# Key weights' low halves behind VectorE's low halves of x, a later table load, and z from two summed tiles

## The chip, the cores and the metric

The kernel runs on one core of a Trainium2 chip. The metric is the time of one execution on the device in microseconds (us), median of a few runs. TensorE multiplies matrices; VectorE, ScalarE and GpSimd work elementwise; SyncE (SP) issues most DMAs, GpSimd some. In the profile they are called PE (PEld: its weight loads), DVE, ACT, POOL and SP. Each engine runs its instructions in order.

## The reference

One transformer block with adaptive layer norm, 2048 rows of 512 numbers in 32 bits. What matters here is the first half:

```python
mod = (_silu(c) @ w_mod).reshape(c.shape[0], 6, 1, -1)
sa, ca, ga, sb, cb, gb = (mod[:, 0], mod[:, 1], mod[:, 2], mod[:, 3], mod[:, 4], mod[:, 5])
h = _layernorm(x, axis=-1) * (1 + ca) + sa
...
phi = lambda t: jnp.where(t > 0, t + 1, jnp.exp(t)) + 1e-6
pq, pk = phi(q), phi(k)
kv = jnp.einsum("bhsd,bhse->bhde", pk, v)
z = jnp.einsum("bhsd->bhd", pk)
num = jnp.einsum("bhqd,bhde->bhqe", pq, kv)
den = jnp.einsum("bhqd,bhd->bhq", pq, z)[..., None] + 1e-6
o = num / den
```

z is the sum of phi(k) over all 2048 rows. Behind this come the projection with wo, the residual, and a second layer norm with two dense layers and Mish, which the change doesn't touch.

## The kernel before

The 2048 rows are four blocks b of four tiles t of 128 rows; the 512 columns are four chunks k of 128. Every matmul operand is split into a high half (h) rounded to TensorE's fast 32-bit type and a low half (l), the remainder; a product takes three matmuls: high by high, high by low, low by high (mm3, L74 to L76). The order of instructions on each engine is the order in which the Python code writes them; waits between engines are put in from the data.

Block 0 is written out by hand (loop at L558 to L610). For each chunk k, ScalarE reads the transposed x from PSUM twice and writes hT_x_0_kh and hf_x_0_k, scaled and shifted by columns k and 4+k of `mc`. VectorE makes those columns with mod_col (L175) and plus_one (L179), and then the low half hT_x_0_kl (L590). GpSimd makes the key weights' halves wk_(k+1)h (a cast, L84) and wk_(k+1)l (a subtraction, L88) one behind the other. ScalarE loads the table that the exponential needs behind the first chunk (L582). TensorE takes hT and wk as they come and sums k = x wk into four PSUM tiles pk_0 to pk_3 (kp in the code).

From pk_t, k_post (L306) lets ScalarE make e_k and relu_k, VectorE ku = min(e_k, 1) + relu_k, and both the halves of ku as pk. g_unit (L327) multiplies normalized x by pk into four PSUM tiles gacc.

The tiles ku are also summed over the blocks for z. Before, four sums ku_0 to ku_3 grow: block 0's tiles are where they begin, blocks 1 and 2 add theirs by a DMA that accumulates in its target, issued by GpSimd (L313), and VectorE adds block 3's (L311). z_unit (L336) then multiplies the four sums by a tile of ones, 32 columns each, into four groups of 32 partitions of one PSUM tile; the two halves of that tile are multiplied by a constant 1/32 later (L683), which adds the partitions up.

Blocks 2 and 3 get x transposed another way: VectorE normalizes (L210) and turns 32 by 32 squares (wide_x, L239), four DMAs write them to DRAM (sq_x<-wide_x) and four read them back (sq_x<-sq_x), and ScalarE scales what comes (hf_x, L270). The layer norm's root is a power on GpSimd (rs_x, L199), between two VectorE steps (L194, and nb_x, L203). For block 3 this is written while block 1 is at work, and its rs_x stands on GpSimd behind the accumulating DMAs of block 1.

Of the kernel before, what the change touches and what calls it, by code (L numbers as in the profile page):

```python
# [13 lines left out]
P = 128  # L14
# [11 lines left out]
def block_kernel(ctx: ExitStack, tc: tile.TileContext, x, wqkv, wo, w1, b1t, w2, c, wmodt, out):  # L26
# [18 lines left out]
    def f32(t):  # L45
        return t.bitcast(F32)
# [21 lines left out]
    def run(gen):  # L68
        for _ in gen:
            pass  # L70

    def mm3(o, st, mv, start, stop):

        pe.matmul(o, st[0], mv[0], start=start, stop=False)  # L74
        pe.matmul(o, st[0], mv[1], start=False, stop=False)  # L75
        pe.matmul(o, st[1], mv[0], start=False, stop=stop)  # L76

    def split(name, t, keep, key, lo_engine=dve, hi_engine=act, plus=None):

# [63 lines left out]
    warm_up(3)  # L143
    ident = cst.tile([P, P], F32, name="ident")
    make_identity(nc, ident)
    w32 = cst.tile([P, P], F32R, name="w32")
    bmask = cst.tile([P, P], F32, name="bmask")
    hmask = cst.tile([P, 4, 32], F32, name="hmask")

    kv = sb("kv")  # L150

    def make_constants():
        pool.memset(f32(w32), 1.0 / 32)
        pool.memset(kv, 0.0)

        pool.memset(bmask, 1.0)
        bm3 = bmask.rearrange("p (a r) -> p a r", r=16)
        pool.affine_select(bm3, bm3, pattern=[[-16, 8], [0, 16]], compare_op=ALU.is_ge,
                           fill=0.0, base=0, channel_multiplier=1)
        pool.affine_select(bm3, bm3, pattern=[[16, 8], [0, 16]], compare_op=ALU.is_ge,  # L160
                           fill=0.0, base=15, channel_multiplier=-1)

        pool.memset(hmask, 1.0)
        pool.affine_select(hmask, hmask, pattern=[[128, 4], [-16, 32]], compare_op=ALU.is_ge,
                           fill=0.0, base=0, channel_multiplier=1)
        pool.affine_select(hmask, hmask, pattern=[[-128, 4], [16, 32]], compare_op=ALU.is_ge,
                           fill=0.0, base=15, channel_multiplier=-1)
# [138 lines left out]
    def k_post(p, b, t, hi_engine=act):  # L306
        u = ku[b, t] = sb(f"ku_{b}_{t}")
        yield from phi(p, f"k_{b}_{t}", u)
        yield from split(f"pk_{b}_{t}", u, pk, (b, t), hi_engine=hi_engine, plus=TINY)
        if b == NB - 1:  # L310
            dve.tensor_tensor(ku[0, t], ku[0, t], ku.pop((b, t)), op=ALU.add)  # L311
        elif b:
            pool.dma_start(ku[0, t], ku.pop((b, t)), accum_op=ALU.add)  # L313

    def k_unit(b, *tiles):
        p = {t: ps("h", f"pk_{b}_{t}") for t in tiles}
# [10 lines left out]
    def g_unit(b, t):  # L327
        if not gacc:
            gacc.extend(ps("acc", f"gacc_{k}") for k in range(4))
        for k in range(4):  # L330
            cs = slice(P * k, P * (k + 1))
            mm3(gacc[k], [h[:, cs] for h in xn[b, t]], pk[b, t], b == 0 and t == 0, b == NB - 1 and t == 3)

    zsum = [sb(f"zsum_{i}", F32R) for i in range(2)]

    def z_unit():  # L336

        p = ps("h", "z")
        for t in range(4):
            pe.matmul(p[32 * t:32 * (t + 1), :], ones[:, 0:32], ku.pop((0, t)), start=True, stop=True)  # L340
        act.activation(zsum[0], p, AF.Copy)
        dve.scalar_tensor_tensor(zsum[1], p, S * TINY / 4, f32(zsum[0]), op0=ALU.add, op1=ALU.subtract)

    def q_unit(b, g):
        p = ps("h", f"pq_{b}_{g}")
# [207 lines left out]
    def step(*gens):  # L553
        for g in gens:
            next(g, None)

    tss = [slice(P * t, P * (t + 1)) for t in range(4)]
    for k in range(4):  # L558
        hi, lo = sb(f"hT_x_0_{k}h", F32R), sb(f"hT_x_0_{k}l", F32R)
# [16 lines left out]
        else:  # L576
            upper(hi, 0, 512)
            upper(hf_k, 0, 512)
        if k < 3:
            run(split(f"wk_{k + 1}", wraw[1, k + 1], wk, k + 1, pool, pool))  # L580
        if k == 0:
            act.preload_act_table_set("exp_and_others")  # L582
            mod_pair(1)
        if k == 1:
            step(xsplit[0])
            mod_col(7, sc_bc)
            plus_one(7, 8)
        if k == 3:
            step(xsplit[0])
        dve.tensor_tensor(lo, hf_k, f32(hi), op=ALU.subtract)  # L590
        if k == 0:
            mod_pair(2)
        if k == 1:
            mod_col(3, sc_bc)
        if k == 0:

            for ts_ in (0, 1), (2, 3):
# [1039 lines left out]
```

## Time and profile before

| | |
|---|---|
| median of 3 runs | 483.81 us (483.48 to 484.19) |
| the profiled execution, whole | 483.39 us |
| its span, first to last instruction | 481.6 us |
| TensorE busy | 474.2 us, 98% of the span |
| VectorE, ScalarE, GpSimd busy | 393.5, 309.3, 128.9 us |
| chain that ended last, by engine | TensorE 85%, VectorE 7%, DMA 3%, ScalarE 2% |

A busy TensorE isn't a TensorE at its peak, since matmuls overlap and their ends are modelled: read the waits. The chain that ended last leads from engine to engine through what released each step. A landing time is that of a DMA from its issue to its last byte's signal.

### The profile page before, as it was taken

The numbers are of one execution on the slowest core, as the hardware profiler recorded it, in microseconds if no ns is written. First come the engines' busy times: TensorE is split into PE (matmuls) and PEld (weight loads), VectorE is DVE, ScalarE is ACT, GpSimd is POOL, SyncE is SP. The second block draws the span as 40 slices with busy tenths as digits, with TensorE's granted clock in tenths as the row PEclk, the third lists the DMA queues.
The fourth block names the chain that finished last, engine by engine and source line by source line (L and its number), as shares of the span: only waits on it lengthen the run. The fifth ranks groups of instructions, "written<-read, shape, count | busy, mean of one in ns | idle before, by whom it ended". The sixth has DMA issues, their size and how long they took to land.

```text
span 481.6 us, 7044 instructions
## 1 busy us (share of the span) xinstructions
PE 474.2 (98%) x2290; PEld 387.6 (80%) x2290; DVE 393.5 (82%) x785; ACT 309.3 (64%) x555; POOL 128.9 (27%) x216
## 2 busy tenths in 40 slices
PE   7999999999999999999999999999999999999997
PEld 6688877768887888788888888888888888888887
DVE  6899898999899889699779873799444787779992
ACT  6786468756667977587787756694166677537700
POOL 3673121000022254112223424343011101354400
PEclk9999999999999999999999999999999999999999
DMA  8904849543766246927538759999543503487964
GB/s 282 389 30 86 198 103 286 180 139 102 242 177 186 94 115 175 323 93 242 174 110 236 246 157 293 376 309 285 182 124 88 112 21 87 110 218 162 240 155 101
DMA packets 83839, 87.00 MB, mean 181 GB/s; under 512 B 23217, under 2 KB 57529, under 8 KB 83802
## 3 DMA queue, kind: packets, MB, share of 16 engines
q1 hardware_dynamic: 58248, 50.22, 34.9%
q0 software_dynamic: 23296, 35.54, 27.0%
q10 hardware_dynamic: 2258, 0.79, 0.7%
q8 instruction: 18, 0.29, 0.2%
q14 instruction: 19, 0.16, 0.1%
HBM read 57.42 MB, written 24.91 MB: 171 GB/s over the span
## 4 chain that ended last, share of the span: by engine, by line
PE 85%; DVE 7%; DMA 3%; ACT 2%; issue 1%; POOL 1%; SPq 0%; DVEq 0%; ACTq 0%
PE p_a L1205 15%; PE o L952 9%; PE p_s L1205 8%; PE oacc L75 5%; PE oacc L76 5%; PE oacc L74 5%; PE m L75 5%; PE m L74 5%; PE m L76 5%; PE p L1205 4%; PE pq_a L390 2%; PE pq L74 2%; DMA sq_x<-wide_x 2%; PE pq L75 2%; PE pq L76 2%; PE pk L76 1%
## 5 line engine op out<-in xcount | busy, mean ns | idle before, releaser
L1210 DVE TENSOR_TENSOR cb<-p_s,u 128x512 f32<-128x512 f32 x28 | 19.2, 687 | 12.2 <-ACT u L1258 10.7
L791 POOL DMA_DIRECT2D wb<-w2d x14 | 9.8, 705 | 65.1 <-PE m L76 28.3
L1197 ACT ACTIVATE ub<-cb,b1c 128x512 f32<-128x512 f32 x28 | 20.0, 719 | 9.0 <-DVE cb L1210 8.7
L1533 POOL DMA_DIRECT2D wt_m<-w2t x20 | 14.0, 702 | 25.2 <-PE m L76 16.9
L1215 ACT ACTIVATE p<-p_a 128x512 f32<-128x512 f32 x12 | 7.0, 582 | 20.9 <-PE p_a L1205 11.7
L199 POOL TENSOR_TENSOR rs_n<-rs_n,half 128x1 f32<-128x1 f32 x16 | 10.2, 636 | 36.9 <-DVE rs_n L225 19.1
L904 POOL DMA_DIRECT2D rden_d<-rden x2 | 1.5, 734 | 61.0 <-DVE rden L902 61.0
L1258 ACT ACTIVATE u<-p_a 128x512 f32<-128x512 f32 x14 | 8.4, 597 | 13.8 <-PE p_a L1205 13.6
L1172 ACT ACTIVATE u<-p,b1c 128x512 f32<-128x512 f32 x14 | 9.6, 685 | 11.7 <-PE p L1205 11.7
L1172 ACT ACTIVATE u<-p_a,b1c 128x512 f32<-128x512 f32 x14 | 9.6, 688 | 8.5 <-PE p_a L1205 8.3
L797 POOL DMA_DIRECT2D w2b<-w2d x20 | 10.6, 544 | 12.8 <-PE oacc L76 4.6
L304 DVE SCALAR_TENSOR_TENSOR ku<-e_k,relu_k 128x512 f32<-128x512 f32 x16 | 10.9, 684 | 1.9 <-ACT relu_k L302 1.9
L199 POOL TENSOR_TENSOR rs_x<-rs_x,half 128x1 f32<-128x1 f32 (+1 forms) x10 | 7.8, 785 | 15.8 <-DVE rs_x L194 14.9
L270 ACT ACTIVATE hf_n<-sq_n,mc 128x512 f32<-128x512 f32 x16 | 12.0, 802 | 0.0
L304 DVE SCALAR_TENSOR_TENSOR q<-e_q,relu_q 128x512 f32<-128x512 f32 x16 | 10.7, 688 | 1.4 <-ACT relu_q L302 1.4
L190 DVE BATCH_NORM_STATS2 st_x<-x 128x6 f32<-128x512 f32 x13 | 8.8, 676 | 3.0 <-DMA x<-in_x_dram 3.0
L301 ACT ACTIVATE e_k<-pk 128x512 f32<-128x512 f32 x16 | 9.4, 590 | 2.5 <-PE pk L76 2.5
L313 POOL DMA_DIRECT2D ku<-ku x8 | 7.2, 938 | 13.8 <-DVE ku L304 13.8
L256 POOL DMA_DIRECT2D sq_n<-wide_n x16 | 8.7, 554 | 7.2 <-DVE wide_n L239 4.7
L916 DVE SCALAR_TENSOR_TENSOR q<-q,rd 128x512 f32<-128x512 f32 x16 | 10.4, 684 | 0.3 <-DMA rd<-rden_d 0.3
L175 DVE SCALAR_TENSOR_TENSOR wm<-wm,sc_row 128x512 f32<-128x512 f32 x16 | 10.5, 685 | 0.0
L730 DVE TENSOR_TENSOR w2g<-w2r,gb_bc 128x256 f32<-128x256 f32 x28 | 10.0, 419 | 0.0
(1612 smaller groups left out, 1880.4 us busy)
## 6 DMA issues: line engine op xcount, KB each, us to landing
wm<-in_wmodt_dram SPq DMA_DIRECT2D x24, 256.0 KB
w1p<-in_w_dram SPq DMA_DIRECT2D x24, 256.0 KB
w2b<-w2d POOLq DMA_DIRECT2D x20, 256.0 KB, 7.3
wt_m<-w2t POOLq DMA_DIRECT2D x20, 256.0 KB, 3.6
r<-in_x_dram SPq DMA_DIRECT2D x16, 256.0 KB
x<-in_x_dram SPq DMA_DIRECT2D x15, 256.0 KB
w2r<-in_w_dram SPq DMA_DIRECT2D x14, 256.0 KB
wb<-w2d POOLq DMA_DIRECT2D x14, 256.0 KB, 3.4
```

Of the source, the lines that this page charges most:

```text
L74: pe.matmul(o, st[0], mv[0], start=start, stop=False)
L75: pe.matmul(o, st[0], mv[1], start=False, stop=False)
L76: pe.matmul(o, st[1], mv[0], start=False, stop=stop)
L199: pool.tensor_tensor(y, y, half[:, lo:hi], op=ALU.pow)
L270: act.activation(dst.rearrange("p (t a i) -> p t a i", t=4, a=4), turned.pop((key, b, j)).rearrange("p (a t i) -> p t a i", a=4, t=4), AF. ...
L304: dve.scalar_tensor_tensor(dst, e, 1.0, r, op0=ALU.min, op1=ALU.add)
L952: pe.matmul(p, l, r, start=not seeded and g == 0 and i == 0, stop=g == 3 and i == 2, skip_group_check=seeded)
L1172: act.activation(u, p, AF.Mish, bias=b1c[:, f:f + 1])
L1197: act.activation(u, p, AF.Mish, bias=b1c[:, f:f + 1])
L1205: pe.matmul(p, st, mv, start=onto is None and c == 0 and i == 0, stop=c == 1 and i == 2, skip_group_check=onto is not None)
L1210: dve.tensor_tensor(out, p, u, op=ALU.add)
L1533: pool.dma_start(v, w2t[g][:, :, SUM[name], :])
```

## The change

Five things. **Gates:** GpSimd's order in block 0 gets three copies of one element, `behind(lo)`, each reading a low half hT_x_0_kl that VectorE writes, so that what stands behind on GpSimd can't begin before that half is done. **Shares:** wk_2h goes from GpSimd to ScalarE, wk_3l from GpSimd to VectorE; xn_0h and xn_0l (halves of normalized x) and the scalings by `mc` move within their engines. **Table:** the load for the exponential moves behind ScalarE's reads of the last chunk. **First g_unit:** its twelve matmuls go over the four gacc tiles with one kind of half after the other, and those with pk_0l last. **z:** two sums grow instead of four. Block 0's tiles 2 and 3 are added by DMA too, tiles t and t + 2 of each block go to the same sum, z_unit has two matmuls of 64 columns, and the constant is 1/64.

```diff
@@ -308,9 +308,11 @@
         if b == NB - 1:
-            dve.tensor_tensor(ku[0, t], ku[0, t], ku.pop((b, t)), op=ALU.add)
+            dve.tensor_tensor(ku[0, t % 2], ku[0, t % 2], ku.pop((b, t)), op=ALU.add)
         elif b:
-            pool.dma_start(ku[0, t], ku.pop((b, t)), accum_op=ALU.add)
+            if b == 1 and t < 2:
+                pool.dma_start(ku[0, t], ku.pop((0, t + 2)), accum_op=ALU.add)
+            pool.dma_start(ku[0, t % 2], ku.pop((b, t)), accum_op=ALU.add)
...
+        if first:
+            (xh, xl), (ph, pl) = xn[b, t], pk[b, t]
+            for n, (l, r) in enumerate(((xh, ph), (xl, ph), (xh, pl))):
+                for k, cs in enumerate(css):
+                    pe.matmul(gacc[k], l[:, cs], r, start=n == 0, stop=False)
+            return
...
-        for t in range(4):
-            pe.matmul(p[32 * t:32 * (t + 1), :], ones[:, 0:32], ku.pop((0, t)), start=True, stop=True)
+        for t in range(2):
+            pe.matmul(p[64 * t:64 * (t + 1), :], ones[:, 0:64], ku.pop((0, t)), start=True, stop=True)
...
+    def behind(t):
+
+        pool.tensor_copy(gate, f32(t)[0:1, 0:1])
...
@@ -576,22 +601,30 @@
-        if k < 3:
-            run(split(f"wk_{k + 1}", wraw[1, k + 1], wk, k + 1, pool, pool))
         if k == 0:
-            act.preload_act_table_set("exp_and_others")
+            wk_upper(1, pool)
             mod_pair(1)
         if k == 1:
+            wk_upper(2, act)
+        if k == 2:
             step(xsplit[0])
-            mod_col(7, sc_bc)
-            plus_one(7, 8)
+        if k == 3:
+            act.preload_act_table_set("exp_and_others")
+        dve.tensor_tensor(lo, hf_k, f32(hi), op=ALU.subtract)
+        if k == 0:
+            behind(lo)
+            wk_lower(1, pool)
+            mod_pair(2)
+        if k == 1:
+            behind(lo)
+            wk_lower(2, pool)
+            wk_upper(3, pool)
+            mod_pair(3)
+        if k == 2:
+            wk_lower(3, dve)
         if k == 3:
             step(xsplit[0])
-        dve.tensor_tensor(lo, hf_k, f32(hi), op=ALU.subtract)
-        if k == 0:
-            mod_pair(2)
-        if k == 1:
-            mod_col(3, sc_bc)
+            behind(lo)
```

wk_upper and wk_lower write a chunk's high and low half of the key weights on the engine that they are given.

How the instructions stand, in three places. First GpSimd in block 0, before; a name in brackets is an engine or a DMA whose signal the instruction waits for:

```order
L84 CAST wk_1h<-wr_1_89 128x512 [waits DMAHW2_49]
L88 TENSOR_TENSOR wk_1l<-wr_1_89,wk_1h 128x512 [waits Pool_49]
L84 CAST wk_2h<-wr_2_95 128x512 [waits DMAHW5_49]
L88 TENSOR_TENSOR wk_2l<-wr_2_95,wk_2h 128x512 [waits Pool_49]
L84 CAST wk_3h<-wr_3_101 128x512 [waits DMAHW0_49]
L88 TENSOR_TENSOR wk_3l<-wr_3_101,wk_3h 128x512 [waits Pool_49]
L84 CAST xn_1h<-x_1_75 128x512 [waits Activation_49]
```

and GpSimd at the same place now:

```order
L577 CAST wk_1h<-wr_1_89 128x512 [waits DMAHW2_49]
L570 COPY gate<-hT_x_0l 1x1 [waits DVE_49]
L580 TENSOR_TENSOR wk_1l<-wr_1_89,wk_1h 128x512 [waits Pool_49]
L570 COPY gate<-hT_x_1l 1x1 [waits DVE_49,Pool_49]
L580 TENSOR_TENSOR wk_2l<-wr_2_95,wk_2h 128x512 [waits DMAHW5_49,Activation_49]
L577 CAST wk_3h<-wr_3_101 128x512 [waits DMAHW0_49]
L570 COPY gate<-hT_x_3l 1x1 [waits DVE_49,Pool_49]
L84 CAST xn_1h<-x_1_75 128x512
```

Each gate reads one of VectorE's low halves; wk_2h and wk_3l have left this engine.

Second, VectorE at the same place, from the low half of chunk 0 to that of chunk 3, before:

```order
L590 TENSOR_TENSOR hT_x_0l<-hf_x_0_194,hT_x_0h 128x512
L175 SCALAR_TENSOR_TENSOR wm_91,mc<-wm_91,sc_bc 128x512
...
L175 SCALAR_TENSOR_TENSOR wm_93,mc<-wm_93,sc_bc 128x512
L175 SCALAR_TENSOR_TENSOR wm_97,mc<-wm_97,sc_bc 128x512
...
L590 TENSOR_TENSOR hT_x_1l<-hf_x_1_243,hT_x_1h 128x512
L175 SCALAR_TENSOR_TENSOR wm_99,mc<-wm_99,sc_bc 128x512
L590 TENSOR_TENSOR hT_x_2l<-hf_x_2_271,hT_x_2h 128x512
L88 TENSOR_TENSOR xn_0l<-x_0_70,xn_0h 128x512
L590 TENSOR_TENSOR hT_x_3l<-hf_x_3_281,hT_x_3h 128x512
```

and VectorE there now:

```order
L613 TENSOR_TENSOR hT_x_0l<-hf_x_0_195,hT_x_0h 128x512
L175 SCALAR_TENSOR_TENSOR wm_91,mc<-wm_91,sc_bc 128x512
...
L175 SCALAR_TENSOR_TENSOR wm_93,mc<-wm_93,sc_bc 128x512
L613 TENSOR_TENSOR hT_x_1l<-hf_x_1_244,hT_x_1h 128x512
L175 SCALAR_TENSOR_TENSOR wm_97,mc<-wm_97,sc_bc 128x512
...
L175 SCALAR_TENSOR_TENSOR wm_99,mc<-wm_99,sc_bc 128x512
L613 TENSOR_TENSOR hT_x_2l<-hf_x_2_273,hT_x_2h 128x512
L580 TENSOR_TENSOR wk_3l<-wr_3_101,wk_3h 128x512
L613 TENSOR_TENSOR hT_x_3l<-hf_x_3_283,hT_x_3h 128x512
L88 TENSOR_TENSOR xn_0l<-x_0_70,xn_0h 128x512
```

Chunk 1's low half stands one scaling earlier, wk_3l is new, and xn_0l stands behind the last low half.

Third, GpSimd in block 1, from the root of block 2's layer norm to that of block 3's, before. DMASW and a number is the signal of one of GpSimd's own DMAs, numbered in turn from 0 with the first row below that is a DMA:

```order
L199 TENSOR_TENSOR rs_x_460<-rs_x_460,half 128x4 [waits DVE_49]
L313 DMA ku_0_314<-ku_0_579 128x512 [waits DVE_49]
L313 DMA ku_1_319<-ku_1_605 128x512 [waits DVE_49]
L313 DMA ku_2_338<-ku_2_633 128x512 [waits DVE_49]
L313 DMA ku_3_343<-ku_3_661 128x512 [waits DVE_49]
L199 TENSOR_TENSOR rs_x_691<-rs_x_691,half 128x4 [waits DVE_49]
L449 DMA ga_d<-ga_row 4x128 [waits Activation_49]
```

and GpSimd there now (ku_2_342 and ku_3_347 are block 0's tiles, ku_0_318 and ku_1_323 the two sums):

```order
L199 TENSOR_TENSOR rs_x_464<-rs_x_464,half 128x4 [waits DVE_49]
L314 DMA ku_0_318<-ku_2_342 128x512
L315 DMA ku_0_318<-ku_0_583 128x512 [waits DMASW0_49,DVE_49]
L314 DMA ku_1_323<-ku_3_347 128x512
L315 DMA ku_1_323<-ku_1_609 128x512 [waits DMASW2_49,DVE_49]
L315 DMA ku_0_318<-ku_2_638 128x512 [waits DMASW1_49,DVE_49]
L315 DMA ku_1_323<-ku_3_667 128x512 [waits DMASW3_49,DVE_49]
L199 TENSOR_TENSOR rs_x_697<-rs_x_697,half 128x4 [waits DVE_49]
L458 DMA ga_d<-ga_row 4x128 [waits Activation_49]
```

Two DMAs more stand ahead of block 3's rs_x, and four of the six wait for the DMA before them onto the same sum.

## Rows read from the trace of the kernel before

**Rows 1.** The page, part 2: TensorE's granted clock in 40 slices, tenths.

```profile
PEclk9999999999999999999999999999999999999999
```

**Rows 2.** Waits of TensorE, whole span: us in total, times, longest.

```profile
PE pk L604 <- DVE hT_x_0l L590: 0.8, 1, 0.8
...
PE gacc L75 <- DVE pk_0l L90: 0.2, 1, 0.2
PE pk L76 <- DVE hT_x_2l L88: 0.2, 1, 0.2
```

**Rows 3.** Windows: length, busy us (instructions) by engine, PEclk, DMA share, GB/s.

```profile
110.00:481.60 371.60, 368.26 (x1824) 304.83 (x1822) 296.53 (x578) 232.83 (x421) 96.40 (x164) 1.00 0.63 179
```

**Rows 4.** Timeline 11 to 21 us: start, us, engine, line, out<-in, idle before.

```profile
11.69 1.27 POOL L88 TENSOR_TENSOR wk_1l<-wr,wk_1h 128x512 fp32r<-128x512 f32 x1
11.73 1.28 ACT L582 ACT_TABLE_LOAD   x1
11.74 1.77 DVE L590 TENSOR_TENSOR hT_x_0l<-hf_x,hT_x_0h 128x512 fp32r<-128x512 f32 x1
...
12.12 0.60 PE L531 MATMUL tp_x<-ident,x 128*128 128x128 f32 x4
...
15.99 1.62 POOL L88 TENSOR_TENSOR wk_3l<-wr,wk_3h 128x512 fp32r<-128x512 f32 x1
...
16.99 1.17 DVE L590 TENSOR_TENSOR hT_x_2l<-hf_x,hT_x_2h 128x512 fp32r<-128x512 f32 x1
...
19.10 0.68 DVE L590 TENSOR_TENSOR hT_x_3l<-hf_x,hT_x_3h 128x512 fp32r<-128x512 f32 x1
...
20.39 0.39 PE L76 MATMUL pk<-wk_3h,hT_x_3l 128*128 128x512 f32 x1
...
20.81 0.60 ACT L301 ACTIVATE e_k<-pk 128x512 f32<-128x512 f32 x1 [1.71 <-PE pk L76]
```

**Rows 5.** Chain that ended last: start, us, what.

```profile
18.71 0.23 PE pk L74
...
43.86 7.59 DMA sq_x<-wide_x
```

**Rows 6.** Timeline of GpSimd, 36.5 to 57 us.

```profile
36.81 1.45 POOL L199 TENSOR_TENSOR rs_x<-rs_x,half 128x4 f32<-128x4 f32 x1
42.86 1.07 POOL L313 DMA_DIRECT2D ku<-ku  x1 [4.60 <-DVE ku L304]
...
50.60 0.86 POOL L313 DMA_DIRECT2D ku<-ku  x1 [2.20 <-DVE ku L304]
56.23 1.04 POOL L199 TENSOR_TENSOR rs_x<-rs_x,half 128x4 f32<-128x4 f32 x1 [4.77 <-DVE rs_x L194]
```

**Rows 7.** Tile ku: landings of all eight; of the one issued at 45.22; at 50.60.

```profile
DMA to landing us min/median/max: 4.7/6.9/9.3
...
DMA to landing us min/median/max: 7.5/7.5/7.5
...
DMA to landing us min/median/max: 5.7/5.7/5.7
```

**Rows 8.** Timeline of VectorE, 57 to 62 us.

```profile
57.30 0.16 DVE L203 SCALAR_TENSOR_TENSOR nb_x<-mv_x,rs_x 128x4 f32<-128x4 f32 x1 [1.16 <-POOL rs_x L199]
...
59.41 0.69 DVE L88 TENSOR_TENSOR hT_x_1l<-hf_x,hT_x_1h 128x512 fp32r<-128x512 f32 x1 [0.43 <-ACT hT_x_1h L82]
...
61.56 0.65 DVE L88 TENSOR_TENSOR hT_x_2l<-hf_x,hT_x_2h 128x512 fp32r<-128x512 f32 x1
```

**Rows 9.** Waits of GpSimd, 0 to 100 us.

```profile
POOL ga_bc L451 <- DMA ga_d<-ga_row: 3.4, 1, 3.4
```

**Rows 10.** Timeline of TensorE around z: 101.5 to 101.7, then 98 to 110 us.

```profile
101.57 0.63 PE L340 MATMUL z<-ku,ones 128*32 128x512 f32 x3
...
101.57 1.90 PE L340 MATMUL z<-ku,ones 128*32 128x512 f32 x8
...
102.42 0.14 PEld L340 LDWEIGHTS z<-ku,ones 128*32 128x32 f32 x2 [0.70 <-DVE ku L311]
```

More of the change, by code (lines that the diff above doesn't have):

```diff
@@ L145, in block_kernel @@
     make_identity(nc, ident)
-    w32 = cst.tile([P, P], F32R, name="w32")
+    w64 = cst.tile([P, P], F32R, name="w64")
     bmask = cst.tile([P, P], F32, name="bmask")
@@ L152, in make_constants @@
     def make_constants():
-        pool.memset(f32(w32), 1.0 / 32)
+        pool.memset(f32(w64), 1.0 / 64)
         pool.memset(kv, 0.0)
@@ L329, in g_unit @@
             gacc.extend(ps("acc", f"gacc_{k}") for k in range(4))
-        for k in range(4):
-            cs = slice(P * k, P * (k + 1))
-            mm3(gacc[k], [h[:, cs] for h in xn[b, t]], pk[b, t], b == 0 and t == 0, b == NB - 1 and t == 3)
+        first = b == 0 and t == 0
+        css = [slice(P * k, P * (k + 1)) for k in range(4)]
+        if first:
[4 more added lines that the diff above has]
+            return
+        for k, cs in enumerate(css):
+            mm3(gacc[k], [h[:, cs] for h in xn[b, t]], pk[b, t], False, b == NB - 1 and t == 3)
     zsum = [sb(f"zsum_{i}", F32R) for i in range(2)]
@@ L338, in z_unit @@
         p = ps("h", "z")
-        for t in range(4):
-            pe.matmul(p[32 * t:32 * (t + 1), :], ones[:, 0:32], ku.pop((0, t)), start=True, stop=True)
+        for t in range(2):
+            pe.matmul(p[64 * t:64 * (t + 1), :], ones[:, 0:64], ku.pop((0, t)), start=True, stop=True)
         act.activation(zsum[0], p, AF.Copy)
-        dve.scalar_tensor_tensor(zsum[1], p, S * TINY / 4, f32(zsum[0]), op0=ALU.add, op1=ALU.subtract)
+        dve.scalar_tensor_tensor(zsum[1], p, S * TINY / 2, f32(zsum[0]), op0=ALU.add, op1=ALU.subtract)
     def q_unit(b, g):
@@ L555, in step, with wk_upper, wk_lower @@
             next(g, None)
+    gate = cst.tile([1, 1], F32, name="gate")
+    def behind(t):
+        pool.tensor_copy(gate, f32(t)[0:1, 0:1])
+    def wk_upper(k, engine):
+        wk[k] = sb(f"wk_{k}h", F32R), sb(f"wk_{k}l", F32R)
+        if engine is act:
+            act.activation(wk[k][0], wraw[1, k], AF.Copy)
+        else:
+            engine.tensor_copy(wk[k][0], wraw[1, k])
+    def wk_lower(k, engine):
+        engine.tensor_tensor(wk[k][1], wraw[1, k], f32(wk[k][0]), op=ALU.subtract)
     tss = [slice(P * t, P * (t + 1)) for t in range(4)]
@@ L682, in z_side @@
         for i in range(2):
-            pe.matmul(zbc_ps, w32, zsum[i], start=i == 0, stop=i == 1)
+            pe.matmul(zbc_ps, w64, zsum[i], start=i == 0, stop=i == 1)
         zbc = sb("zbc_sb")
```

## The prediction

> **What bounds the kernel now.** Read first the granted clock: it is full in all forty slices [rows 1], so every matmul time below is at the 2.4 GHz level. Then read whom TensorE waits for. Behind the first 24 us there is one listed wait, of 0.2 us, for a low half of block 2 [rows 2]. Behind that wait none is listed, and from 110 us on TensorE is busy 368.26 of 371.60 us [rows 3]. So whatever moves TensorE's first 62 us moves the end of the kernel by as much, and the change touches nothing behind 104 us. The question is only by how much TensorE is earlier or later at that wait for hT_x_2l of block 2, at 62.2 us.
>
> Two stretches decide that. In the **start** (11 to 21 us), VectorE's hT_x_0l takes 1.77 us where hT_x_3l, with nobody beside it, takes 0.68; GpSimd runs wk_1l in that time [rows 4], and TensorE waits 0.8 us [rows 2]. The same shows at hT_x_2l, 1.17 us beside wk_3l [rows 4]. In **blocks 1 to 2** (42 to 62 us), the chain runs through the turned block's way out to DRAM (7.59 us [rows 5]) and back and through VectorE, which at 57.30 has waited 1.16 us for GpSimd's rs_x and then has 4.9 us of work up to the end of hT_x_2l, with one hole of 0.43 us [rows 8]. That rs_x (of block 3) stands on GpSimd behind the four accumulating DMAs of block 1, at 56.23, and began when VectorE's input came [rows 6].
>
> **The change, part by part.**
>
> *Gates and the shared low halves.* The gate puts wk_1l behind hT_x_0l. hT_x_0l then runs 11.74 to 12.42 (0.68, not 1.77), and TensorE, which is done with its transposes at 12.72, goes on there and not 0.8 later. At 0.23 us a matmul [rows 5] the 19th matmul from there, the first that needs hT_x_2l, would start at 12.72 + 18 x 0.23 = 16.86, and the 28th, the last of pk_0, at 18.93 where it now starts at 20.39 [rows 4]. So 1.5 us is the most that the start can give. I take less, because the low halves still meet. VectorE has two scalings of about 0.7 us and a small step behind hT_x_0l, to 13.9; wk_1l (1.27) runs from about 12.7, the gate's own time included, to 14.1; hT_x_1l follows to 14.8; wk_2l from about 15.1 to 16.4. hT_x_2l is free to run at about 16.2 and meets wk_2l's end, and then perhaps the cast wk_3h: its end falls at 17.1 to 17.7, against TensorE's 16.86. From that matmul pk_0 needs nine more steps, 2.1 us: last start 19.2 to 19.8, a gain of 0.6 to 1.2. I take **0.9 us**; the ends are 1.5 and 0 (the collision comes back in full elsewhere). The gates themselves (1x1 copies, of which no row has a like) are inside these figures, as 0.1 to 0.6 us each.
>
> *wk_2h on ScalarE, wk_3l on VectorE, order of the scalings.* ScalarE's copy (about 0.6) lies where its table load (1.28) was. wk_3l (0.68) lies on VectorE ahead of hT_x_3l, before TensorE has reached pk_0's last three matmuls. Nothing of its own.
>
> *Table load.* It moves behind hf_x_3, which ends near 17.8; 1.28 and the copy sc_row (0.6) bring ScalarE to 19.7, and pk_0 is complete at 19.4 to 20.2. ScalarE waits 1.71 us there now [rows 4], which is its cover. Zero, at most 0.3 late, inside the range of the 0.9.
>
> *Order of the first g_unit.* TensorE no longer waits for pk_0l there (0.2 us [rows 2]), but the chain runs over ScalarE and VectorE here and TensorE only gets further ahead. Zero.
>
> *z with two matmuls.* Three of the four column groups start together at 101.57; the fourth waits for VectorE's last sum to 102.42 and takes the rest alone, to 103.47 [rows 10]. With two groups the second waits for the same sum and ends at the same time: zero. If the eight passes went one after another (1.90 us, 0.24 each), four fewer would save 0.95; that is the other end. By the Trainium skill, page "TensorEngine Tiling (Array Packing)", section Key Properties, different tiles run matmuls in parallel, so fewer and wider groups should save nothing. The rows agree with it; the sum by the other reading would be 0.95 lower.
>
> *The accumulating DMAs.* This is the term that I weigh most. Two tiles instead of four mean two DMAs more in block 1, and every DMA onto a tile waits for the one before it onto the same tile. GpSimd is in order, so such a wait holds everything behind it, as ga_bc's wait of 3.4 us for ga_d shows [rows 9], and here what stands behind is rs_x of block 3. Count from T, the issue of ku_0's own block-1 accumulate (42.86 now). The first extra DMA (ku_2 onto ku_0) has no wait, follows the rs_x that ends at 38.26, and has landed by about T if it takes the least that one took, 4.7 [rows 7]. The second (ku_3 onto ku_1) issues at T + 1.07. ku_1's own accumulate waits for it to land. Its nearest row is the second accumulate of now, which lies as it does behind the first one and behind the block's store: 7.5. Then ku_0's next one needs no more waiting, and the last (ku_3 of block 1 onto ku_1) waits for ku_1's own to land; nearest row the one issued at 50.60, beside the load: 5.7 [rows 7]. Its issue takes 0.86. So rs_x starts at T + 1.07 + 7.5 + 5.7 + 0.86 + 0.1 = T + 15.2; with the median landing, 6.9, twice, T + 15.8. Now it starts at 56.23 = T + 13.4. The added wait is 1.8 to 2.4; I take **2.2**. Both landings at the least, 4.7, give T + 11.4, earlier than VectorE has its input: no delay. 7.5 and 7.9 would give 4.0. Behind rs_x wait nb_x of block 3, VectorE's two scalings of x and hT_x_0l of block 2, and with that TensorE.
>
> *Given back.* VectorE's hole of 0.43 us at hT_x_1l goes, since ScalarE's halves are then early: -0.4.
>
> **The sum.** T moves with the start. -0.9 (start) + 2.2 (GpSimd's wait) - 0.4 (hole) = +0.9 us. Span and rest of the profiled execution are 483.39 us, so 484.3 there; it lies 0.4 below the median of the three runs, 483.81, so **484.7** for the median. That is close to the bound of what can be told from no change, 0.2% or 0.97 us.
>
> **The rivals.**
>
> *The landings are short and the start's gain comes through.* If both waits end within VectorE's time (each landing below about 5.7), rs_x starts as soon as VectorE gives its input, and with the hole gone the result is -0.9 - 0.4 = -1.3: 482.5. For it: the shortest landing is 4.7, and fewer accumulates compete with the load of block 2 now, since two wait. Against: the second extra DMA is queued behind another one and behind the store (7.59 us [rows 5]).
>
> *TensorE's clock falls in the new wait: slower.* In the forecast TensorE stands still about 2.5 us in front of hT_x_0l of block 2: rs_x is 1.3 late in absolute time, and TensorE is 1.2 early. Nothing like it is in the trace, where the longest wait of rows 2 is 0.8 and the clock is full throughout [rows 1]. At the lower of its two levels, 1.2 GHz, a matmul takes 0.46 and not 0.23, so that each us of TensorE's work costs another; 2 us of work done at that level give +0.9 + 2 = +2.9: 486.7. It decides as soon as the granted clock shows below 1.00 between 58 and 66 us. The Trainium skill, page "TensorE: Matmul & The Clock Gate", section "HAM oscillation — how this bites in real kernels", says that idle gaps between bursts bring the clock down; no run here shows it. Landings longer than I took (the 7.9 case, +2.7) end at the same place without it.
>
> *The gates bring nothing.* The low halves of wk meet hT_x_1l and hT_x_2l instead, and e_k starts as now, at 20.81: 0 + 2.2 - 0.4 = +1.8, 485.6. Against it speaks that the 0.8 us wait for hT_x_0l [rows 2] has nothing left to make it.
>
> **How the numbers follow.** Forecast 0.5: its own spread, about 0.6 us each way from the landings and the start, lies half above +0.97, so 0.24 slower and 0.26 the same. Short landings 0.2: 0.17 faster, 0.03 the same. Clock or long landings 0.18, all slower. Gates without gain 0.12: 0.09 slower, 0.03 the same. Faster 0.17, same 0.32, slower 0.51. The range leaves a tenth on each side: down to 482.6, which takes in most of the short landings, and up to 486.4, which takes in the gates without gain and the lower part of the slow cases.
>
> **What would show it.** Right: hT_x_0l of block 0 at 0.7 us, first e_k near 19.9; on GpSimd six accumulates between 36 and 57 us with waits named for ku DMAs, and rs_x of block 3 starting near 57 to 58; nb_x waiting for rs_x about 3 us or more, and TensorE idle in front of hT_x_0l of block 2; z ending one pass pair behind VectorE's last sum. Wrong: rs_x waiting for VectorE as now (then the time is near 482.5); e_k still at 20.8; or z's end moved forward against that sum.

## The result and the profile after

| | before | after |
|---|---|---|
| median, run side by side (9 runs each) | 483.48 us (482.47 to 484.29) | 486.03 us (484.24 to 487.40) |
| ratio after to before | | 1.0044, 95% interval 1.0025 to 1.0064 |
| the profiled execution, its span | 483.39, 481.6 us | 484.46, 482.7 us |
| TensorE, VectorE, ScalarE, GpSimd busy | 474.2, 393.5, 309.3, 128.9 us | 473.5, 392.2, 310.0, 129.4 us |

Slower by 0.44%, inside the range. (The ratio is that of the means, which the two groups below pull apart; by the medians it is 0.53%.) The nine times of after are two groups, told apart by TensorE's mean granted clock, which each run records: four at 0.999 to 1.000 (484.24, 484.46, 484.46, 484.89) and five at 0.995 or 0.996 (486.03, 486.27, 486.37, 486.57, 487.40). Before has one group: 88 runs of it beside the experiments are all at 0.999 or 1.000. The profiled execution is of the first group, so the trace of after shows the loss without the clock's part: its span is 1.1 us longer.

**The start** (timeline of after, 11 to 20 us; columns: start, duration, engine, line, operation, operands, count, and in brackets the idle time ahead and what ended it). These lines answer [rows 4].

```profile
11.62 0.69 DVE L613 TENSOR_TENSOR hT_x_0l<-hf_x,hT_x_0h 128x512 fp32r<-128x512 f32 x1
12.38 0.18 POOL L570 COPY gate<-hT_x_0l 1x1 f32<-1x1 f32 x1 [0.74 <-DVE hT_x_0l L613]
...
17.32 1.28 ACT L612 ACT_TABLE_LOAD   x1
...
19.14 0.60 ACT L301 ACTIVATE e_k<-pk 128x512 f32<-128x512 f32 x1
```

The gate does what it should: hT_x_0l takes 0.69 us and not 1.77, and the first e_k starts at 19.14 where it started at 20.81. ScalarE has no idle time ahead of that e_k, since the table load and sc_row run up to it. They hardly hold it: pk_0's last matmul starts at 18.71 (before 20.39), and the 0.42 us that lay before between that start and e_k would put e_k at 19.13 too.

**GpSimd in block 1** (timeline of after, same columns; L314 is a new DMA of block 0's tiles, L315 block 1's own). These lines answer [rows 6].

```profile
36.46 1.07 POOL L314 DMA_DIRECT2D ku<-ku  x1
41.71 0.89 POOL L315 DMA_DIRECT2D ku<-ku  x1 [4.18 <-DVE ku L304]
42.27 1.21 POOL L314 DMA_DIRECT2D ku<-ku  x1
51.34 1.74 POOL L315 DMA_DIRECT2D ku<-ku  x2 [7.86 <-DVE st_x L190]
56.73 0.86 POOL L315 DMA_DIRECT2D ku<-ku  x1 [3.65 <-DMA ku<-ku]
57.30 1.36 POOL L199 TENSOR_TENSOR rs_x<-rs_x,half 128x4 f32<-128x4 f32 x1
```

Nothing is issued from 43.5 to 51.3: ku_1's own accumulate waits there for the extra one onto ku_1. The profile names a VectorE step as releaser, but that step writes nothing that these DMAs read, and the tile that the first of them adds had been ready for some 7 us (with z undone, below, its DMA goes at 44.38). Then the last one waits 3.65 us for ku_1's own, and rs_x of block 3 stands behind it.

**VectorE and TensorE behind it** (timeline of VectorE; then TensorE's waits from 20 to 130 us: total, times, longest; then the windows from 57 us: busy time of each engine, granted clock PEclk, DMA share, GB/s). They answer [rows 8], [rows 2] and [rows 1].

```profile
54.82 0.17 DVE L194 TENSOR_SCALAR rs_x<-mv_x 128x4 f32<-128x4 f32 x1
58.69 0.16 DVE L203 SCALAR_TENSOR_TENSOR nb_x<-mv_x,rs_x 128x4 f32<-128x4 f32 x1 [3.69 <-POOL rs_x L199]
59.68 0.69 DVE L88 TENSOR_TENSOR hT_x_0l<-hf_x,hT_x_0h 128x512 fp32r<-128x512 f32 x1
62.42 0.65 DVE L88 TENSOR_TENSOR hT_x_2l<-hf_x,hT_x_2h 128x512 fp32r<-128x512 f32 x1
```

```profile
PE pk L76 <- DVE hT_x_0l L88: 2.7, 1, 2.7
```

```profile
58.00:59.00 1.00, 0.00 (x0) 0.00 (x0) 0.31 (x2) 1.00 (x2) 0.65 (x1) 1.00 1.04 305
59.00:60.00 1.00, 0.00 (x0) 0.00 (x0) 1.00 (x3) 0.97 (x3) 0.00 (x0) 1.00 1.16 326
```

VectorE waits 3.69 us for rs_x, and hT_x_2l of block 2, the place where the kernel before waited last, comes 0.86 us later than before (62.42 against 61.56). TensorE stands still for two whole windows. In this execution the granted clock stayed full all the same. The profile's own chain names another releaser for hT_x_0l, ScalarE's hT_x_2h, which ends at the same moment, 59.68; hT_x_0l doesn't read it, and VectorE is at work without a gap from nb_x on. In the kernel with the wait alone, below, the chain does run over rs_x and nb_x.

**z** (timeline of TensorE in after; answers [rows 10]): four passes and not eight, and the next product starts 1.90 us behind the first pass, where it was 1.82 before.

```profile
102.44 1.97 PE L349 MATMUL z<-ku,ones 128*64 128x512 f32 x4
104.34 0.50 PE L74 MATMUL gacc<-pk_3h,xn_3h 128*128 128x512 f32 x1
```

### The profile page after: what moved, and what is told of

Read it like the earlier page. It is cut to its first block, busy times and chain, and to the rows that moved or that the text cites. A ratio compares the mean times of both kernels' runs of the same rounds, so it can differ in the third digit from the quotient of the medians.

```text
span 482.7 us, 7051 instructions
## 1 busy us (share of the span) xinstructions
PE 473.5 (98%) x2286; PEld 387.3 (80%) x2286; DVE 392.2 (81%) x786; ACT 310.0 (64%) x556; POOL 129.4 (27%) x219
## 4 chain that ended last, share of the span: by engine, by line
PE 79%; DVE 9%; DMA 6%; ACT 2%; SPq 1%; POOL 1%; issue 1%; ACTq 0%
PE p_a L1238 15%; PE p_s L1238 8%; PE oacc L75 5%; PE oacc L74 5%; PE oacc L76 5%; PE o L985 5%; PE m L75 5%; PE m L76 5%; PE m L74 5%; PE p L1238 4%; DMA sq_x<-wide_x 3%; PE pq_a L399 2%; PE pq L74 2%; PE pq L76 2%; PE pq L75 2%; PE gacc L75 1%
## 5 line engine op out<-in xcount | busy, mean ns | idle before, releaser
L315 POOL DMA_DIRECT2D ku<-ku x8 | 7.0, 956 | 21.1 <-DVE st_x L190 7.9
L304 DVE SCALAR_TENSOR_TENSOR ku<-e_k,relu_k 128x512 f32<-128x512 f32 x16 | 10.9, 683 | 1.2 <-ACT relu_k L302 1.2
L949 DVE SCALAR_TENSOR_TENSOR q<-q,rd 128x512 f32<-128x512 f32 x16 | 10.4, 683 | 0.4 <-DMA rd<-rden_d 0.3
L270 ACT ACTIVATE hf_x<-sq_x,mc 128x512 f32<-128x512 f32 x8 | 6.4, 806 | 5.5 <-DMA sq_x<-sq_x 5.5
```

Of the source, the lines that this page charges most:

```text
L270: act.activation(dst.rearrange("p (t a i) -> p t a i", t=4, a=4), turned.pop((key, b, j)).rearrange("p (a t i) -> p t a i", a=4, t=4), AF. ...
L304: dve.scalar_tensor_tensor(dst, e, 1.0, r, op0=ALU.min, op1=ALU.add)
```

## The experiments

Theory **W**: the loss is GpSimd's rs_x behind waiting accumulates, and the clock falls on TensorE's gap that follows. Rivals: **S**, the new start costs; **D**, the DMAs' traffic costs, whoever waits. Every execution of every kernel below ran at 0.999 or 1.000 unless the text says otherwise. Ratios are to the kernel before on the same chip.

### The parts apart

z undone: in the changed kernel, four sums again.

```diff
-            if b == 1 and t < 2:
-                pool.dma_start(ku[0, t], ku.pop((0, t + 2)), accum_op=ALU.add)
-            pool.dma_start(ku[0, t % 2], ku.pop((b, t)), accum_op=ALU.add)
+            pool.dma_start(ku[0, t], ku.pop((b, t)), accum_op=ALU.add)
...
-            pe.matmul(p[64 * t:64 * (t + 1), :], ones[:, 0:64], ku.pop((0, t)), start=True, stop=True)
+            pe.matmul(p[32 * t:32 * (t + 1), :], ones[:, 0:32], ku.pop((0, t)), start=True, stop=True)
```

> The changed kernel with its z part undone: four summed tiles again, one accumulating DMA per tile in block 1, everything else of the change kept. Theory W (the loss is GpSimd's rs_x of block 3, which stands behind accumulates that wait for one another): no accumulate waits for a landing, rs_x starts when VectorE gives its input, near 55.1 us, VectorE's nb_x waits about 1 us as before, and the start's gain is left: 1.1 to 1.6 us below the kernel before, near 482.3, with a granted clock of 0.999 or more in every execution. Theory S (the gates and moved low halves cost what was lost): no faster than the kernel before, 483.5 or more. Theory D (what is lost is bandwidth that the two extra DMAs take from the block's store): as W here, so this run does not tell W and D apart.

Measured: 483.13 us (11 runs), ratio 0.9995 (0.9987 to 1.0004). rs_x starts at 55.38, as W wants, and yet nothing is gained: a miss for W's number. S's number is near (before ran at 483.16 on that chip), but S itself, a start that costs, doesn't follow: nothing is lost either, and the start's steps come nearly as early as in after (first e_k at 19.41). The gain was lost in the DMAs. The lines below are of this kernel: the step of the chain that is the turned block's store (start, duration), SyncE's store (L245) and load (L266) with their issue times, and VectorE at block 2's first halves.

```profile
43.10 8.16 DMA sq_x<-wide_x
```

```profile
41.14 3.40 SPq L245 DMA_DIRECT2D sq_x<-wide_x  x4
51.41 2.97 SPq L266 DMA_DIRECT2D sq_x<-sq_x  x4
```

```profile
57.72 0.69 DVE L88 TENSOR_TENSOR hT_x_0l<-hf_x,hT_x_0h 128x512 fp32r<-128x512 f32 x1 [0.18 <-ACT hT_x_0h L82]
59.09 0.69 DVE L88 TENSOR_TENSOR hT_x_1l<-hf_x,hT_x_1h 128x512 fp32r<-128x512 f32 x1 [0.68 <-ACT hT_x_1h L82]
```

The store begins 0.8 us earlier than before and lands at about the same time (8.16 us, before 7.59 [rows 5]), the load's first tile is only 0.3 earlier, and VectorE, which has rs_x in time, now has holes of 0.18 and 0.68 where there was one of 0.43 [rows 8].

z alone: the same edit the other way round, put into the kernel before.

> The kernel before with the z part of the change alone: two summed tiles, two accumulating DMAs more in block 1; the start as before. Theory W: ku_0's block-1 accumulate stays at 42.9, rs_x of block 3 starts 15.6 us behind it, near 58.5 (before 56.2), TensorE stands still 2 to 3 us in front of block 2's hT_x_0l, and the time is 2.0 to 2.5 us above the kernel before where the clock stays full (485.6 to 486.1), and about 2 us more in executions where it falls. Theory S: within 0.3 us of the kernel before (483.2 to 483.8).

Measured: 484.14 us (11 runs), ratio 1.0022 (1.0012 to 1.0032). W's number is missed: about half of what it wanted. In the trace the accumulates wait less (6.45 and 2.13 us), and rs_x is not late at all; what is late is the store, 8.85 us in the chain. GpSimd's lines:

```profile
50.48 1.71 POOL L315 DMA_DIRECT2D ku<-ku  x2 [6.45 <-DVE xn_3l L88]
54.31 0.86 POOL L315 DMA_DIRECT2D ku<-ku  x1 [2.13 <-DMA ku<-ku]
55.65 1.04 POOL L199 TENSOR_TENSOR rs_x<-rs_x,half 128x4 f32<-128x4 f32 x1 [0.48 <-DVE rs_x L194]
```

So the start alone gives nothing, z alone costs 1.0 us, and both together cost 1.0 us at the full clock, no more than the sum; what goes beyond it is the clock's fall. The way is another one, though: z alone costs by a late store (in its trace hT_x_2l comes at 61.90, 0.34 later than before), which is nearer to rival D, while the wait of rs_x and the gap on TensorE are there only when both are.

### The wait and the clock

The wait alone, without the two DMAs: z undone as above, and GpSimd kept busy ahead of rs_x.

```diff
+                if b == 3:
+                    spare = sb("spare")
+                    pool.tensor_copy(spare[:, 0:4], rs["x", b])
+                    for i in range(3):
+                        pool.memset(spare, 0.0)
                 ln_rstd("x", b)
```

> The changed kernel with z undone (483.1, full clock) and, on GpSimd, a small copy of VectorE's input and three memsets of 128x512 ahead of rs_x of block 3, about 1.9 us: the wait of the changed kernel without its two DMAs. Theory W (the wait is what costs, and TensorE's standing still behind it is what the clock falls on): rs_x near 57.3, nb_x waits about 3 us, TensorE stands still 2 to 2.7 us ahead of hT_x_0l, 484.0 to 484.8 in executions with the granted clock at 0.999 or more, and some near 486 with 0.996. Theory D (the two extra DMAs' traffic makes the loss, the wait is covered): 483.0 to 483.5 and no execution below 0.999.

Measured: 485.69 us, ratio 1.0036 (1.0021 to 1.0050), in two groups as in after: five executions at 0.999 or 1.000 (483.61 to 484.57, median 483.92) and six at 0.996 (485.69 to 486.86, median 485.8). W holds, with the first group at the low edge of its number and TensorE standing still for 1.66 us, less than the 2 to 2.7 expected. The profiled execution is of the second group, so here the fall can be seen (GpSimd's lines; TensorE's lines around the gap; windows as above):

```profile
55.39 1.70 POOL L485 MEMSET spare<- 128x512 f32 x3
57.06 1.04 POOL L199 TENSOR_TENSOR rs_x<-rs_x,half 128x4 f32<-128x4 f32 x1
```

```profile
57.81 0.40 PE L75 MATMUL pk<-wk_0l,hT_x_0h 128*128 128x512 f32 x1
59.86 0.53 PE L76 MATMUL pk<-wk_0h,hT_x_0l 128*128 128x512 f32 x1 [1.66 <-DVE hT_x_0l L88]
```

```profile
58.00:59.00 1.00, 0.20 (x1) 0.00 (x0) 0.87 (x3) 0.97 (x3) 0.10 (x1) 1.00 0.01 4
59.00:60.00 1.00, 0.14 (x1) 0.14 (x2) 1.00 (x3) 0.97 (x2) 0.00 (x0) 1.00 0.00 0
60.00:61.00 1.00, 1.00 (x3) 0.81 (x4) 1.00 (x3) 0.97 (x3) 0.00 (x0) 0.60 0.00 0
61.00:62.00 1.00, 1.00 (x4) 0.76 (x3) 1.00 (x3) 0.52 (x1) 0.00 (x0) 0.50 0.00 0
62.00:63.00 1.00, 1.00 (x4) 0.81 (x3) 1.00 (x2) 0.00 (x0) 0.00 (x0) 0.50 0.00 0
63.00:64.00 1.00, 1.00 (x4) 0.77 (x4) 1.00 (x3) 0.00 (x0) 0.00 (x0) 0.70 0.00 0
64.00:65.00 1.00, 1.00 (x7) 0.79 (x6) 1.00 (x3) 0.00 (x0) 0.00 (x0) 1.00 0.00 0
```

PEclk is full while TensorE stands still, falls when work comes back at 60 us, and is full again at 64. 0.50 is the lower of the two levels, 1.2 GHz. The lost share is 0.4 + 0.5 + 0.5 + 0.3 = 1.7 us; the two groups lie 1.9 us apart, here and in after (486.37 against 484.46). This is the only trace with the fall in it; that the other executions of the second group lost their clock in the same place is not shown, only that they have the same mean.

The gap filled: the changed kernel, with matmuls that nobody reads in TensorE's gap.

```diff
             elif t == 0:
+                if b == 2:
+                    fill = ps("tp", "fill")
+                    for i in range(9):
+                        pe.matmul(fill[:, P * (i % 4):P * (i % 4 + 1)], ones, ones, start=True, stop=True)
                 posts = k_unit(b, 0, 1)
```

> The changed kernel with nine matmuls of 128 columns, ones by ones into a spare tile whose result nobody reads, on TensorE just ahead of block 2's first matmul, where it stands still 2.7 us; they take about 2.4 us. If the standing still makes the granted clock fall in some executions: every execution now at 0.999 or more and near 484.2 to 484.9 (or a few tenths above, if the filler outlasts the wait), and none near 486.4. If the clock falls for another reason: two groups of times as in the changed kernel, some near 484.5 with clock 0.999 and about half near 486.4 with 0.996.

Measured: 484.39 us, all eight runs between 484.10 and 485.01 at 0.999 or 1.000; ratio 1.0028 (1.0017 to 1.0039). The second group is gone, and the first stays where it was. One listed wait of half a microsecond is left of the gap:

```profile
60.13 0.50 PE L76 MATMUL pk<-wk_0h,hT_x_0l 128*128 128x512 f32 x1 [0.51 <-DVE hT_x_0l L88]
```

### The accumulates and the store

Both extra DMAs early: the same six accumulates on the same tiles.

```diff
-            if b == 1 and t < 2:
-                pool.dma_start(ku[0, t], ku.pop((0, t + 2)), accum_op=ALU.add)
+            if b == 1 and t == 0:
+                for i in range(2):
+                    pool.dma_start(ku[0, i], ku.pop((0, i + 2)), accum_op=ALU.add)
```

> The changed kernel with both extra DMAs (ku_2 onto ku_0, ku_3 onto ku_1) issued together at 36.5 us, behind block 1's first tile; the same six DMAs on the same tiles, only the second extra one 4 us sooner, so that it has landed when ku_1's own accumulate comes. Theory W: no or little waiting on GpSimd, ku_1's accumulate near 45, the last one near 51 to 54, rs_x of block 3 near 55, the time 0.9 to 1.6 us below the kernel before (482 to 482.6), clock 0.999 or more. Theory D (the extra DMAs cost by the bandwidth that they take, wherever they stand): rs_x near 55 too, but block 1's way out and back late, and the time no better than the kernel before, 483.5 to 484.5.

Measured: 482.29 us (11 runs), ratio 0.9978 (0.9970 to 0.9987): W, and faster than both kernels. GpSimd's lines:

```profile
36.66 2.11 POOL L315 DMA_DIRECT2D ku<-ku  x2
41.96 0.85 POOL L316 DMA_DIRECT2D ku<-ku  x1 [3.18 <-DMA ku<-ku]
44.33 0.86 POOL L316 DMA_DIRECT2D ku<-ku  x1 [1.51 <-DVE ku L304]
49.88 0.85 POOL L316 DMA_DIRECT2D ku<-ku  x1 [4.70 <-DVE ku L304]
52.95 0.86 POOL L316 DMA_DIRECT2D ku<-ku  x1 [2.23 <-DVE wm L175]
55.35 1.04 POOL L199 TENSOR_TENSOR rs_x<-rs_x,half 128x4 f32<-128x4 f32 x1 [1.54 <-DVE rs_x L194]
```

rs_x no longer waits for them. D, that the two extra DMAs cost wherever they stand, is out; beside the store they do, as z alone shows. But this kernel beats the one with z undone by 0.8 us, which W alone can't explain: there no accumulate waits either. What differs is that two of the four accumulates come 3 us later here (49.88 and 52.95, against 46.72 and 49.75). The store gains nothing by that: from its first issue to the load's it takes 10.4 us, with z undone 10.3. It is the load that is shorter. Its four issues take 1.81 us and not 2.97, and its first tile is there 1.6 us earlier than with z undone (56.20):

```profile
54.62 0.82 ACT L270 ACTIVATE hf_x<-sq_x,mc 128x512 f32<-128x512 f32 x1 [4.52 <-DMA sq_x<-sq_x]
```

Whether the accumulates' place is what counts: the kernel with z undone, with block 1's accumulates behind rs_x.

```diff
-            pool.dma_start(ku[0, t], ku.pop((b, t)), accum_op=ALU.add)
+            if b == 1:
+                late.append(t)
+            else:
+                pool.dma_start(ku[0, t], ku.pop((b, t)), accum_op=ALU.add)
...
                 ln_rstd("x", b)
+                if b == 3:
+                    for t in late:
+                        pool.dma_start(ku[0, t], ku.pop((1, t)), accum_op=ALU.add)
```

> The changed kernel with z undone (four accumulates in block 1) and these four issued only behind rs_x of block 3, near 56 to 60 us, so that none of them moves bytes beside the turned block's store and load (42 to 57 us). Theory Q (store, load and accumulates share DMA engines that are full from 43 us on, and so the start's gain ends at the store's landing): the store lands 2 us or more before the 51.3 of the kernel with z undone, the first hf_x starts by 54 (there 56.2), VectorE's holes of 0.18 and 0.68 at hT_x_0l and hT_x_1l go, and the time is 0.8 to 1.4 us below the kernel with z undone: 481.8 to 482.4. Theory L (store and load take that long by themselves): store landing near 51.3 again and the time near 483.1.

Measured: 481.87 us (7 runs, 481.76 to 482.45), ratio 0.9971 (0.9960 to 0.9982), 1.3 us below the kernel before: theory Q, and the best of all versions. (`late` is a list made ahead of this.) SyncE's lines, ScalarE's first tile of the load, and a window (as above):

```profile
41.37 3.40 SPq L245 DMA_DIRECT2D sq_x<-wide_x  x4
48.44 1.76 SPq L266 DMA_DIRECT2D sq_x<-sq_x  x4
```

```profile
51.11 0.82 ACT L270 ACTIVATE hf_x<-sq_x,mc 128x512 f32<-128x512 f32 x1 [0.77 <-DMA sq_x<-sq_x]
```

```profile
48.00:50.00 2.00, 2.00 (x11) 1.65 (x10) 2.00 (x5) 1.09 (x3) 0.00 (x0) 1.00 0.26 61
```

From the store's first issue to the load's first issue it takes 7.1 us, where it takes 10.3 with z undone and accumulates in the way. The DMA engines' share at 48 to 50 us is 0.26; with z undone it is 1.03, and in the kernel before it was 1.02:

```profile
48.00:50.00 2.00, 2.00 (x11) 1.65 (x10) 2.00 (x6) 1.43 (x3) 0.40 (x1) 1.00 1.02 195
```

The first hf_x is 5.1 us earlier, and VectorE has no hole left.

The late accumulates in the kernel before, with nothing of the change:

> The kernel before with one thing changed: block 1's four accumulates are issued behind rs_x of block 3. No part of the change is in it. If both the later accumulates and the new start have a worth of their own: the turned block is back before VectorE wants it, the hole of 0.43 goes, 0.4 to 0.7 us below the kernel before (482.5 to 482.8), and 0.6 to 0.9 above the same with the new start (481.9). If the accumulates' place is all of it and the start is worth nothing: 481.7 to 482.1, as with the new start.

Measured: 482.95 us (12 runs; before 483.46 on that chip), ratio 0.9986 (0.9975 to 0.9998). Both have a worth: later accumulates 0.5 to 0.7 us, and the new start, once nothing is in its way, the difference of the ratios 0.9986 and 0.9971, about 0.7 us. Their intervals overlap a little.

The late accumulates with all of the change, both extra DMAs early:

> All parts of the change, with the two extra DMAs issued early, at 36.5 us, and block 1's four accumulates behind rs_x of block 3: nothing of z's new sums lies in the way of rs_x, the store or the load. What z itself is worth shows against the kernel with four sums and late accumulates (481.9). Theory zero (z's fourth group waits for VectorE's sum either way): 481.7 to 482.2. If half the passes were worth time: 480.9 to 481.2. If the four accumulates, two by two onto one tile, wait for each other and hold ga_d and ga_bc behind them until somebody wants those: above 482.4.

Measured: 482.88 us (11 runs; before 483.46 on that chip), ratio 0.9983 (0.9973 to 0.9994). Relative to before it is 0.6 us dearer than the kernel with four sums and late accumulates, though the intervals overlap. z's two sums save nothing, which the z lines show too (1.85 us from the first pass to the next product, 1.87 with four sums). The number is that of the third expectation, but not its mechanism: two accumulates wait 1.87 and 0.63 us, and ga_d goes at 64.08, no later than elsewhere. hT_x_2l of block 2 is even earlier (60.04, against 60.39), z later (100.86, against 100.39): some 0.8 us are lost between them. A line of ScalarE in block 3 has them:

```profile
84.11 0.63 ACT L82 ACTIVATE hT_x_3h<-hf_x 128x512 fp32r<-128x512 f32 x1 [0.79 <-DMA ku<-ku]
```

With four sums this hT_x_3h starts at 83.69 without a wait. It reads nothing that an accumulate writes, so it can only be waiting for its buffer, which an accumulate of block 2 still reads; that is argued from the code. And that accumulate is late by the two sums: block 2's third one waits for the first onto the same sum and goes at 75.46, with four sums at 72.25. So two by two they do wait for one another, and it does cost, one block later than the expectation had it.

### The start

The start undone: the kernel before with z and both extra DMAs early.

> The kernel before with the z part, both extra DMAs early, and nothing else of the change: the start, table load and first gram product as before. If the start's gain reaches the end once the store's and the accumulates' traffic no longer collide: 0.7 to 1.0 us above the 482.3 of the same kernel with the new start, so 483.0 to 483.3, rs_x of block 3 near 56.2. If the new start is worth nothing at the end: 482.1 to 482.5.

Measured: 482.89 us (11 runs), ratio 0.9988 (0.9978 to 0.9998). The new start is worth 0.6 us there by the medians (482.29 with it), 0.5 by the ratios, whose intervals overlap; a little under the expected 0.7 to 1.0.

The gates taken out of the kernel with both extra DMAs early (`behind` does nothing), and out of the kernel with late accumulates:

> The changed kernel with both extra DMAs early (482.3 there), without the three 1x1 copies on GpSimd that hold the key weights' low halves behind VectorE's. Theory G (the gates make the start's gain): hT_x_0l takes 1.3 to 1.8 us again and not 0.7, the first e_k starts 0.5 us or more behind 19.1, and the time is 0.5 to 1 us more: 482.8 to 483.3. Theory T (the order on ScalarE and VectorE and the moved table load make it, and the gates nothing): e_k within 0.2 us of 19.1, time 482.1 to 482.5.

> The changed kernel with z undone, block 1's accumulates late (481.9), and without the three 1x1 copies that hold the key weights' low halves: what the gates are worth where no DMA is in the way. Theory G (gates worth 0.3 to 0.7): 482.2 to 482.6. Theory T (they are worth nothing, the low halves only meet one step elsewhere): 481.7 to 482.0, and the first e_k no later than 0.2 us against the end of hT_x_0h's work.

Measured: 482.94 us, ratio 0.9993 (0.9984 to 1.0002), against 0.9978 with gates; and 483.28 us (before 483.46 on that chip), ratio 0.9995 (0.9985 to 1.0005), against 0.9971. The gates are worth 0.7 and 1.2 us by these ratios (the first pair's intervals overlap a little), and without them nothing of the start's gain is left (482.94, against 482.89 with the whole start undone): the rest of the start alone has no worth that these runs show. How the gates do it is shown less well, since each side has one trace and where the halves meet changes from execution to execution. In the second trace theory G's signs are there: hT_x_1l took 1.67, the first e_k came at 20.36 (with gates 19.65), and the loss goes through to block 2's hT_x_2l (61.09, against 60.39) and z (101.09, against 100.39). In the first, G has only its time. VectorE's hT_x_0l came through in 0.69, GpSimd's half took 1.63, and e_k came as with the gates (19.33), which are theory T's signs; z is 0.58 late, of which 0.50 is the wait of block 3's hT_x_3h for an accumulate. So in that trace the loss is not the start's. Lines of the first, then of the second:

```profile
11.96 1.63 POOL L581 TENSOR_TENSOR wk_1l<-wr,wk_1h 128x512 fp32r<-128x512 f32 x1
...
19.36 0.60 ACT L301 ACTIVATE e_k<-pk 128x512 f32<-128x512 f32 x1
```

```profile
13.95 1.67 DVE L619 TENSOR_TENSOR hT_x_1l<-hf_x,hT_x_1h 128x512 fp32r<-128x512 f32 x1
```

## Why the prediction was right, and where it wasn't

The sign, the place and the range were right, and at the full clock the path and the sum were too. Wrong was what each part is worth by itself; and the median is that of a rival.

- **The sum, in the trace of after.** +0.9 was forecast for the full clock, where +1.0 was measured. Follow the path from ku_0's own accumulate, T. T came 1.15 earlier (41.71, before 42.86; forecast 0.9). rs_x started at T + 15.6, between the 15.2 and 15.8 of the sum, where it was T + 13.4 (+2.2, as forecast). From rs_x to nb_x it took 0.3 more, which the sum lacks, mostly since rs_x itself took 1.36 and not 1.04; from nb_x to hT_x_2l 0.5 less (the hole, forecast 0.4). That makes hT_x_2l 0.86 later, and TensorE's first matmul with it 1.0 later (lines of before, then of after):

```profile
62.26 0.50 PE L76 MATMUL pk<-wk_2h,hT_x_2l 128*128 128x512 f32 x1 [0.20 <-DVE hT_x_2l L88]
```

```profile
63.28 0.39 PE L76 MATMUL pk<-wk_2h,hT_x_2l 128*128 128x512 f32 x1
```

- **GpSimd's wait, +2.2.** The mechanism was right to the step: two waits for landings, rs_x behind them, nb_x behind rs_x (3.69 us), TensorE in front of hT_x_0l (2.68 us). That T + 15.6 came out so near is partly luck: the first landing was longer than its nearest row (8.5 to 9 us from issue, 7.5 taken), the second shorter (about 5, 5.7 taken). And with the old start the same two landings left rs_x in time (z alone). What the wait costs depends on what would have been there without it: 0.8 us put into the kernel with z undone, where 0.86 us of VectorE's holes go under it; about 2 us against the kernel with both extra DMAs early, which has the same six DMAs and no wait of rs_x for them (482.29).
- **Start, -0.9.** In this pair of traces e_k came 1.67 us earlier; over all traces the new start with its gates has e_k at 19.00 to 19.65 (seven), the old one at 20.12 to 20.81 (four), 1.2 us apart in the mean. Of the 1.67 only 1.15 reached T: VectorE's nb_x at 25.35 waited 0.45 us for a GpSimd rs_x that took 1.06, before 0.55. What failed is that this gain moves TensorE's first 62 us by itself, as the rival with short landings has it (-0.9 - 0.4 = -1.3). With z undone no accumulate waits, and the kernel gained nothing (483.13): the store and the accumulates fill the DMA engines from 43 us on, and the store's landing stays at 51.3. The 7.59 us of the chain [rows 5] were taken for a length that moves with T; before's own DMA share of 1.02 at 48 to 50 us speaks against that. In after it does move T, at the head of the path; but z alone costs the same 1.0 us, so the kernel is no better for it there either.
- **Hole, -0.4.** It goes, but not because ScalarE's halves are early: with the start alone the holes were 0.18 + 0.68. It goes when the load is early (481.87) or when rs_x is so late that it covers it, as in after.
- **The parts.** Taken one by one, start and hole give 0 where the sum has -1.3, and z gives +1.0 where the sum has +2.2, by another way than the one forecast. The two errors, of 1.2 to 1.3 us, cancel in the whole.
- **The clock rival** (+2 us on top, 0.18 with the long landings) came true in five of nine executions, at 1.9 us, and so the median 486.03 is its number (486.7) more than the forecast's; with four of nine it would have been 484.89, close to the forecast. That it comes in the place named, behind TensorE's gap, is seen in the one trace that has it, of the kernel with the wait alone. That it depends on the gap is shown: filled, none of eight; made without the DMAs, six of eleven; in kernels without the gap, none. I gave it too little: it needed no long landings, only the 2.5 us of standing still that the forecast itself had. What the Trainium skill says, page "TensorE: Matmul & The Clock Gate", section "HAM oscillation — how this bites in real kernels", that idle gaps between bursts bring the clock down, the windows of the kernel with the wait alone bear out (0.50 to 0.70 from 60 to 64 us, behind the gap), but only for some executions of the same program.
- **Gates, table, g_unit, z.** By the times the gates carry the start's gain, and shares, table and g_unit together show no worth without them; none of the three was run by itself. The gate itself took 0.17 to 0.51 us. z's passes saved nothing, as the rows with the column groups side by side had said; that its two sums make block 3 wait, as with both extra DMAs early and late accumulates, was not foreseen.

Open: why the same gap brings the clock down in one execution and not in the next; and by what way the gates' 0.7 us come in the kernel with both extra DMAs early.

## What to carry to other kernels

Before a start's gain is carried through to the end, look at the DMA share of the stretches in between: a store whose engines are full lands when the bytes are through, not a fixed time behind its issue. Accumulating DMAs that nobody wants soon belong behind the transfer that is on the path, and never ahead of a short instruction that others wait for on an in-order queue; two onto one tile are a wait. A gap that opens on a full TensorE is to be priced with the clock's fall as a likely case, and matmuls that fill it cost nothing here (484.39, against 484.46 unfilled at the full clock).

## What the runs showed of the hardware

- One program had two times, 1.9 us apart, in executions of the same kernel: with a gap on TensorE of 1.7 to 2.7 us, 11 of 20 over two kernels had a mean granted clock of 0.995 or 0.996, the others 0.999 or 1.000. The one trace of the lower kind has 4 us at 0.50 to 0.70 right behind the gap.
- An accumulating DMA of 256 KB landed 3.4 us behind its issue ahead of the store (the one at 36.46 in after) and 5.3 to 8.7 beside the store or the load; from the store's first issue to the load's it took 6.7 to 7.1 us with no accumulates beside the store and 8.9 to 10.9 with them.
- Two 128x512 subtractions on VectorE and GpSimd at the same time took from 0.69 and 1.63 to 1.77 and 1.27 us, and which of the two paid changed between executions.
